# RWKV-7 attention with a hardswish feed-forward: third blocks of a group's inverses made in one unit instead of two

## Chip, cores and metric

The kernel runs on one core of one Trainium2 chip. The metric is the device time of one execution in microseconds (us). Each kernel is run several times; the median is given with the lowest and highest run. The profile comes from one further execution, whose own time is given beside its span. TensorE, VectorE, ScalarE, GpSimd and SyncE are called PE, DVE, ACT, POOL and SP, as in the profile; a line number such as L804 is one of the kernel before.

## The reference, cut to what matters

Attention with a state of 40 x 40 for each of 4 x 8 heads runs over 768 time steps; its output feeds a feed-forward layer from 320 to 2048 and back to 320 features. All data are float32.

```python
B, H, S, D = r.shape                     # 4, 8, 768, 40
for t in range(S):
    y[:, :, t] = einsum('bhd,bhde->bhe', rt, state)
    Sa = einsum('bhde,bhe->bhd', state, at)
    state = state * wt[:, :, None, :] - einsum('bhd,bhe->bhde', Sa, bt)
    state = state + einsum('bhd,bhe->bhde', vt, kt)
x = y.transpose(0, 2, 1, 3).reshape(B * S, H * D)     # 3072 x 320
h = x @ w_in                                          # 3072 x 2048
out = (h * clip(h + 3, 0, 6) / 6) @ w_out             # 3072 x 320
```

## The kernel before

**Units and groups.** The time axis is cut into blocks of 64 steps. A unit is one such block for two of the four batch entries, all 8 heads: it fills 128 partitions with two halves of 64 time steps. There are 24 units, in six groups of four (`NU = 4`). In each half of a unit, the 64 steps depend on each other through a triangular 64 x 64 matrix per head; its inverse `tinv` lets a unit be done with matmuls instead of step by step. The state is carried from unit to unit.

**The inverses.** They are made for a whole group at once, for 4 x 8 heads. `invert` (L744 on) takes the matrix `F` (written by ACT at L657 and L660), and inverts the two diagonal blocks of 32 x 32 on DVE, in some 60 small steps, dealt out one at a time by `aside` between other work. Its results are `tb` and, transposed, `tt`; the two diagonal blocks are copied into `tinv` at once (L790, L791). What is left is the third block, off the diagonal: a product of three 32 x 32 matrices, one after the other. That is `third_block` (L794 on). Each call serves two units of the group, 16 heads. Its first half is 32 small matmuls on PE, `F` times `tb` (L804), into a pair of PSUM banks, which ACT then copies to `zs` in four copies of 32 x 256 (L812). Its second half is 32 small matmuls of `tt` with `zs` (L827) into another pair of banks, copied by ACT into `tinv` in four copies (L837). In the trace each of these matmuls is two records, so that a set of 32 is a row of 64. Each half is a generator step: it yields once after its matmuls (`PE`), and once after its copies (`DONE`). `third_blocks` makes two of them, so that a group has four sets of matmuls and sixteen copies.

**The order of the work.** The instruction order of each engine is the order of the program text: the kernel schedules by hand. From the second group on, a unit is worked in four blocks (`BLOCKS = 4`, `j` from 0 to 3). `a_block` issues the attention stages of the current unit (`OWN_STAGES`) and those that prepare later units (`AHEAD_STAGES`), several stages together: first the matmuls of all, then the copies of all. `feed` puts pieces of the feed-forward of earlier units between them: `expand` (L1124, with `gt` made by ACT at L1139 and DVE at L1140) and `contract` (L1165). At the end of blocks 0 and 1 of the first two units of a group, `block` issues one half of a third block. `aside(3 * L)` before it runs what is left of `invert`. The stages that the prediction's steps touch, by block of a unit, are:

| block | stages and lines |
|---|---|
| 0 | RT and VT: R and V turned (L496, ACT L862, L895) |
| 1 | S (L906, ACT L911), R (PE L884, DVE L888), C (PE L524, DVE L546); with them A and B of a later unit (L496, DVE L615, L623) |
| 2 | U (L925, ACT L929) and UT (L964, ACT L970), which read `tinv`, and rS (L980, ACT L986); with them F, K of a later unit (L650, L486, L670, ACT L679) |
| 3 and 4 | H (L524), ysn (L1021, DVE L1028, L1032) |

The first unit needs the `tinv` of its own heads at block 2, thus one block after the second call of `block`.

**The banks.** PSUM has eight banks here: one called `one`, one `o`, two `h` for the feed-forward, and two pairs called `pair` (`ps_pair`, L141 on), which nearly all stages use in turn. A pair is taken again when its reader has emptied it, so a matmul into a pair waits for the copies of an earlier stage. `ps_pair` gives consecutive calls the same pair while both fit into its 512 columns and `shared[0]` has not been reset; a set of third-block matmuls takes 256 columns.

Of the kernel before, what the change touches and what calls it, by code (L numbers as in the profile page):

```python
# [20 lines left out]
L = 32  # L21
# [10 lines left out]
def kernel(  # L32
# [47 lines left out]
    NU = 2 * NP  # L80
# [762 lines left out]
    def third_blocks(first=False):  # L843

        zs = inv.tile([P, 2, 2, H, L], F32, name="zs", tag="x", bufs=1)
        return [third_block(*third[-1], 2 * n, zs[:, n], first) for n in range(2)]
# [360 lines left out]
    def aside(n, weight=0):  # L1207

        for _ in range(n):
            if side and next(side[0], side) is side:  # L1210
                side.popleft()
            due[0] += weight
            while due[0] >= 1:
                due[0] -= 1
                next(weights, None)

    def deal(n):

        for _ in range(n):
            next(weights, None)  # L1220

    def run(stage, steps=0, mixed=0, deals=0):

        for at in stage:
            if at == DONE:
                return
            aside(steps, mixed)
            deal(deals)
# [71 lines left out]
    blocks = {}  # L1300
# [28 lines left out]

    def block(i, j):  # L1330

        if i % NU < 2:
            if j == 0:
                if i % NU == 0:
                    blocks[i], blocks[i + 1] = third_blocks()
            run(blocks[i])

# [115 lines left out]
    def a_block(m):  # L1455

        if coming and begins[coming[0]] == m:
            u = coming.popleft()
            close = coming and begins[coming[0]] < m + BLOCKS
            ahead[u, m] = prepared(u), CLOSE_STAGES if close else AHEAD_STAGES  # L1460
        if m % BLOCKS == 0 and m // BLOCKS + NU < NK:
            i = m // BLOCKS + NU
            own[i, m] = step(i), OWN_STAGES
        parts = {}, {}
        for (u, begin), (fs, order) in sorted(own.items()) + sorted(ahead.items()):
            if m - begin < len(order):
                for name in order[m - begin]:
                    parts[begin % BLOCKS > 0].setdefault(name, []).append(fs[name])
        for k, part in enumerate(parts):
            together(part)  # L1470
            if any(u % NU == NU - 1 and m - begin == 2 and k == (begin % BLOCKS > 0)
                   for u, begin in ahead):
                third.clear()
                side.append(invert(group_F[-1], third))
            yield

    def feed(n, inversion):

        whole = int(n)
        for k in range(whole):  # L1480
            pieces(1)
            aside(inversion)
        pieces(n - whole)
# [3 lines left out]
    for i in range(NU, NK):  # L1487
        spread[0] = i >= 2 * NU - 1
        for j in range(BLOCKS):
            rate, inversion = 3.5, 0  # L1490
            if i + AHEAD >= NK + NU - 1:
                rate = 4.5
            if i < 2 * NU - 1:
                rate = 2.8
            parts = a_block(m)
            next(parts)
            if side or i % NU == NU - 1 and rate < 4:

                rate, inversion = 6.2, 2 + (i < 2 * NU)
            feed(rate / 2, inversion)  # L1500
            for _ in parts:
                pass
            if i % NU < 2 and j < 2:
                if i % NU == 0:
                    aside(3 * L)
                block(i, j)
            if side:
                rate, inversion = 6.2, 2 + (i < 2 * NU)
            feed(rate / 2, inversion)
            m += 1  # L1510
# [37 lines left out]
```

## Time and profile before

| | |
|---|---|
| median of 3 runs | 786.57 us (786.24 to 786.66) |
| profiled execution | 785.4 us |
| its span in the trace | 783.7 us |
| PE busy | 725.0 us, 93% of the span |
| DVE, ACT, POOL busy | 486.6, 320.2, 171.9 us |
| feed-forward matmuls L1124 and L1165 | 248.7 and 230.5 us busy, in 2304 and 768 records |
| third-block matmuls into `pair` (L804, L827) | 640 and 768 records of 0.19 us, overlapping |
| third-block copies (L812, L837) | 48 and 48 copies of 0.375 us |

A row of the timeline gives the start in us from the begin of the span, how long the row lasts from the start of its first to the end of its last instruction, the engine, the line, the operation, the tiles written and read, the shape, and the number of records that follow each other. A number in brackets is the time that the engine was idle ahead of the row, with the engine that ended it. Records of PE overlap, so the time that a row costs PE is from its start to the start of the next. The row of the stretches gives the length of the stretch, busy time of PE, of its weight load, and of DVE, ACT and POOL with their counts, then the granted clock, the DMA share and the bandwidth.

### The profile page before, as it was taken

The numbers are of one execution on the slowest core, as the hardware profiler recorded it, in microseconds if no ns is written. First come the engines' busy times: TensorE is split into PE (matmuls) and PEld (weight loads), VectorE is DVE, ScalarE is ACT, GpSimd is POOL, SyncE is SP. The second block draws the span as 40 slices with busy tenths as digits, with TensorE's granted clock in tenths as the row PEclk, the third lists the DMA queues.
The fourth block names the chain that finished last, engine by engine and source line by source line (L and its number), as shares of the span: only waits on it lengthen the run. The fifth ranks groups of instructions, "written<-read, shape, count | busy, mean of one in ns | idle before, by whom it ended". The sixth has DMA issues, their size and how long they took to land.

```text
span 783.7 us, 32780 instructions
## 1 busy us (share of the span) xinstructions
PE 725.0 (93%) x14552; PEld 613.3 (78%) x14552; DVE 486.6 (62%) x951; ACT 320.2 (41%) x664; POOL 171.9 (22%) x321
## 2 busy tenths in 40 slices
PE   5636788999999989999999999999999999999998
PEld 3625677878878778888788888888888888888886
DVE  7899967688546699345888336887436972223110
ACT  2386865324445334443334543334543234412211
POOL 6403111222232304121304212203212111110000
PEclk9855899999999999999999999999999999999999
DMA  9684554311333312223213223213221101110000
GB/s 123 116 202 123 113 168 69 68 27 35 58 59 63 67 33 48 50 49 66 41 38 58 46 51 64 44 30 60 49 55 39 26 5 30 30 29 10 12 20 18
DMA packets 174205, 44.87 MB, mean 57 GB/s; under 512 B 157424, under 2 KB 172784, under 8 KB 174064
## 3 DMA queue, kind: packets, MB, share of 16 engines
q1 hardware_dynamic: 169760, 42.03, 27.5%
q8 instruction: 115, 1.88, 1.0%
q10 hardware_dynamic: 4304, 0.74, 0.6%
q14 instruction: 26, 0.21, 0.1%
HBM read 34.08 MB, written 3.93 MB: 49 GB/s over the span
## 4 chain that ended last, share of the span: by engine, by line
PE 77%; DVE 10%; issue 6%; DMA 2%; ACT 2%; POOL 2%; SPq 1%; POOLq 0%; ACTq 0%; DVEq 0%
PE h L1124 27%; PE o L1165 25%; PE pair L1021 4%; PE pair L524 4%; PE pair L496 2%; PE one L486 2%; DVE prods L571 2%; PE pair L884 2%; PE pair L925 1%; PE pair L717 1%; DVE prod L769 1%; PE pair L964 1%; DVE x L775 1%; PE pair L980 1%; PE one L906 1%
## 5 line engine op out<-in xcount | busy, mean ns | idle before, releaser
L1124 PE MATMUL h<-xt,win 128*128 128x128 f32 (+1 forms) x2304 | 248.7, 281 | 4.5 <-DVE gt L1140 4.5
L1124 PEld LDWEIGHTS h<-xt,win 128*128 128x128 f32 (+1 forms) x2304 | 229.3, 191 | 22.6 <-issue 4.2
L1165 PE MATMUL o<-wout,gt 128*128 128x320 f32 x768 | 230.5, 443 | 0.0
L1165 PEld LDWEIGHTS o<-wout,gt 128*128 128x128 f32 x768 | 138.4, 190 | 50.9 <-issue 0.2
L1140 DVE SCALAR_TENSOR_TENSOR gt<-gt,h 128x512 f32<-128x512 f32 x96 | 62.0, 680 | 73.4 <-ACT gt L1139 73.4
L1139 ACT ACTIVATE gt<-h,three 128x512 f32<-128x512 f32 x96 | 62.9, 687 | 102.8 <-PE h L1124 102.3
L546 DVE COPY_PREDICATED area<-mask,pair 128x512 f32<-128x512 int32 x56 | 40.4, 724 | 62.2 <-PE pair L524 52.8
L769 DVE TENSOR_TENSOR prod<-x 128x30 f32<-128x30 f32 (+9 forms) x180 | 65.5, 364 | 8.9 <-POOL x L754 3.3
L775 DVE TENSOR_TENSOR x<-x,prod 128x30 f32<-128x30 f32 (+9 forms) x180 | 64.3, 357 | 5.5
L1029 POOL TENSOR_TENSOR yg<-ys,gam 128x512 f32<-128x512 f32 x20 | 25.4, 1272 | 126.1 <-DVE ys L1028 83.2
L690 POOL TENSOR_TENSOR KBt<-K,rgt 128x320 f32<-128x320 f32 x22 | 19.1, 870 | 151.4 <-ACT rgt L679 139.9
L571 DVE TENSOR_TENSOR_SCAN prods<-area,start 128x528 f32<-128x528 f32 x24 | 40.8, 1703 | 9.7 <-ACT area L567 9.6
L1028 DVE TENSOR_TENSOR ys<-pair,ys 128x512 f32<-128x512 f32 x20 | 13.8, 690 | 49.8 <-PE pair L1021 40.8
L862 ACT ACTIVATE RT<-pair 128x512 f32<-128x512 f32 x22 | 13.1, 597 | 54.5 <-PE pair L496 54.4
L722 ACT ACTIVATE EV<-pair 64x320 f32<-64x320 f32 x44 | 18.9, 430 | 36.9 <-PE pair L717 36.5
L1021 PE MATMUL pair<-area,KBt 64*64 64x104 f32 x1280 | 33.1, 252 | 0.0
L1183 ACT ACTIVATE ob<-o 128x320 f32<-128x320 f32 x22 | 9.6, 437 | 56.2 <-PE o L1165 37.8
L837 ACT ACTIVATE tinv<-pair 32x256 f32<-32x256 f32 x48 | 18.0, 375 | 34.7 <-PE pair L827 34.2
L582 DVE TENSOR_TENSOR_SCAN area<-area,start 128x528 f32<-128x528 f32 x24 | 31.1, 1297 | 0.8
L1021 PEld LDWEIGHTS pair<-area,KBt 64*64 64x64 f32 x1280 | 29.1, 133 | 1.4
L950 POOL COPY area<-V 128x320 f32<-128x320 f32 x20 | 9.1, 455 | 84.6 <-DVE area L612 52.9
L600 POOL COPY rgam<-prods 128x256 f32<-128x256 f32 x22 | 24.9, 1131 | 0.0
(286 smaller groups left out, 1049.9 us busy)
## 6 DMA issues: line engine op xcount, KB each, us to landing
V<-in_v_dram SPq DMA_DIRECT2D x96, 40.0 KB
out_dram<-ob SPq DMA_DIRECT2D x47, 80.0 KB
R<-in_r_dram SPq DMA_DIRECT2D x92, 40.0 KB
B<-in_b_dram SPq DMA_DIRECT2D x42, 80.0 KB
K<-in_k_dram SPq DMA_DIRECT2D x42, 80.0 KB
W<-in_w_dram SPq DMA_DIRECT2D x37, 80.0 KB
A<-in_a_dram SPq DMA_DIRECT2D x37, 80.0 KB
xt<-yg SPq DMA_DIRECT2D x72, 40.0 KB
```

Source lines behind the costliest of these rows:

```text
L524: nc.tensor.matmul(out=o[i][half(q), n ^ (2 * q * placed), :], lhsT=lhs[half(i, D), n ^ (2 * q * swap), half(q)], rhs=rhs[half(i, D), n, h ...
L546: nc.vector.copy_predicated(out=x[:].rearrange("p (i h) t -> p i h t", i=2), mask=mask8, data=o[2])
L571: nc.vector.tensor_tensor_scan(out=prods[:].rearrange("p r m i -> p (r m i)"), data0=wm[:, 0:SCAN], data1=start[:], initial=0.0, op0=ALU.m ...
L582: nc.vector.tensor_tensor_scan(out=back, data0=back, data1=start[:], initial=0.0, op0=ALU.mult, op1=ALU.add)
L769: nc.vector.tensor_tensor(out=pv, in0=_ap(x[:], (i + 1) * L + i, [[L, n], [0, i]]), in1=_ap(x[:], i * L, [[0, n], [1, i]]), op=ALU.mult,)
L775: nc.vector.tensor_tensor(out=rest, in0=rest, in1=pv, op=ALU.add)
L1021: nc.tensor.matmul(out=both[q][half(s), pr, :], lhsT=o[name][half(q), h * D:h * D + SLOT], rhs=beside[name][half(q), 4 * rs + 2 * (s ^ (q ...
L1029: nc.gpsimd.tensor_tensor(out=yg[:], in0=m["ys"][:].rearrange("p r q t -> p r (q t)"), in1=o["G"][:], op=ALU.mult)
L1124: nc.tensor.matmul(out=hp[c][:, i, :], lhsT=lhsT, rhs=rhs, start=(begun[c] == 0), stop=(begun[c] == 3 * NQ - 1))
L1139: nc.scalar.activation(out=gt[:], in_=hp[c][:], func=AF.Relu, bias=three[:], scale=1.0)
L1140: nc.vector.scalar_tensor_tensor(out=gt[:], in0=gt[:], scalar=6.0, in1=hp[c][:], op0=ALU.min, op1=ALU.mult)
L1165: nc.tensor.matmul(out=op[:], lhsT=gts[c][:, n, :], rhs=wout[:, c * HJ + r * NQ + n, :], start=((split or r == 0) and c == 0 and n == 0), ...
```

## The change

Both third blocks of a group are now made in the first unit: behind its block 0 the first halves of both, behind its block 1 the second halves. The matmuls of both come first, then the copies of both. The second unit has none. In the first unit PE thus issues 64 matmuls in a row at L804 and 64 at L827, and ACT eight copies in a row at L812 and eight at L837. Both sets fit into one pair of banks, so that each half takes one pair for four units where it took one for two. The first group, whose third blocks are made elsewhere, is not touched.

```diff
     def block(i, j):
 
-        if i % NU < 2:
-            if j == 0:
-                if i % NU == 0:
-                    blocks[i], blocks[i + 1] = third_blocks()
-            run(blocks[i])
+        if j == 0:
+            blocks[i] = third_blocks()
+        for x in blocks[i]:
+            next(x)
+        for x in blocks[i]:
+            run(x)
...
-            if i % NU < 2 and j < 2:
-                if i % NU == 0:
-                    aside(3 * L)
+            if i % NU == 0 and j < 2:
+                aside(3 * L)
                 block(i, j)
```

## Prediction

> **What bounds the kernel now.** I read the page first (busy shares, slices, chain of waits), then the busy time by stretches, then the timelines of TensorE (PE), ScalarE (ACT) and VectorE (DVE) around every third block (L804, L827), and last the order and the waits of the two programs as built, which hold no times.
>
> ```profile
> PE 725.0 (93%) x14552; PEld 613.3 (78%) x14552; DVE 486.6 (62%) x951; ACT 320.2 (41%) x664; POOL 171.9 (22%) x321
> PE 77%; DVE 10%; issue 6%; DMA 2%; ACT 2%; POOL 2%; SPq 1%; POOLq 0%; ACTq 0%; DVEq 0%
> ```
> ```profile
> 418.00:533.00 115.00, 113.97 (x2382) 97.46 (x2379) 75.50 (x148) 47.53 (x107) 27.26 (x48) 1.00 0.26 49
> ```
> PE carries the chain, and in the stretch of one group (418 to 533 us) it is busy 113.97 of 115.00 us at full granted clock. PE works in order, so what counts is how long its own list of matmuls is, plus each place where the next matmul waits. ACT is busy 41%: its share hides nothing here, since what matters is when its copies end.
>
> The third group shows what the change touches. First unit, PE and then ACT (start, us, what):
> ```profile
> 422.75 0.75 PE L804 MATMUL pair<-tb,F 32*32 32x32 f32 x64
> 423.43 1.16 PE L1124 MATMUL h<-xt,win 128*128 128x128 f32 x8
> ...
> 425.60 0.68 PE L884 MATMUL pair<-state,at 40*64 40x40 f32 x32
> ...
> 426.69 2.42 PE L1165 MATMUL o<-wout,gt 128*128 128x320 f32 x8
> 429.04 0.75 PE L827 MATMUL pair<-zs,tt 32*32 32x32 f32 x64
> ...
> 432.42 0.65 PE L980 MATMUL pair<-RT,S 40*64 40x64 f32 x32
> ```
> ```profile
> 423.66 1.54 ACT L812 ACTIVATE zs<-pair 32x256 f32<-32x256 f32 x4 [2.73 <-PE pair L804]
> 425.22 1.27 ACT L1139 ACTIVATE gt<-h,three 128x512 f32<-128x512 f32 x2
> ...
> 429.84 1.56 ACT L837 ACTIVATE tinv<-pair 32x256 f32<-32x256 f32 x4 [2.86 <-PE pair L827]
> ```
> Look at the margins. The zs copies end at 425.20, and L884, which is built to wait for them (it takes their two banks), starts at 425.60: 0.40 us to spare. The tinv copies end at 431.40, and L980, which takes the banks of L827, starts at 432.42: 1.02 us. Second unit, PE:
> ```profile
> 446.22 1.34 PE L1165 MATMUL o<-wout,gt 128*128 128x320 f32 x4
> 447.49 0.75 PE L804 MATMUL pair<-tb,F 32*32 32x32 f32 x64
> 448.18 1.34 PE L1165 MATMUL o<-wout,gt 128*128 128x320 f32 x4
> 449.36 1.05 PE L1124 MATMUL h<-xt,win 128*128 128x128 f32 x8
> ...
> 453.45 1.16 PE L1124 MATMUL h<-xt,win 128*128 128x128 f32 x8
> 454.87 0.74 PE L827 MATMUL pair<-zs,tt 32*32 32x32 f32 x64 [0.26 <-DVE area L612]
> 455.54 2.05 PE L1124 MATMUL h<-xt,win 128*128 128x128 f32 x16
> 457.43 0.60 PE L486 MATMUL one<-ident,K 128*128 128x128 f32 x4
> ```
> Here each block costs PE its 0.68 us and cuts a run of large matmuls in two.
>
> **The change, part by part.** Five groups (third blocks at about 192, 307, 423, 538 and 650 us). In the built order only PE and ACT differ; DVE, POOL and SP issue the same list, so no DMA moves in its queue.
>
> *Added in the first unit.* L804 and L827 are 128 records each instead of 64. Of the 0.75 us of a set, its last record is 0.19, so 63 steps take 0.56, 8.9 ns each: 64 more cost 0.57. Two per group: +1.14.
>
> *Taken out of the second unit.* Third group: 446.22 to 449.36 is 3.14 us; the same eight L1165 records without a break take 2.35 (426.69 to 429.04), so 0.79 goes. 453.45 to 457.43 is 3.98; 24 records of L1124 without a break take 2.88 (a piece of the chain of waits), so 1.10 goes, the 0.26 of waiting among it. The same way: second group 0.78 (329.59 to 333.80 against 3.43 for twelve) and 1.09; fourth 0.79 and 0.78; fifth 0.68 and 0.77; first 0.68 and 0.68, and 0.12 more where L980 at 228.28 waited for tinv copies that ended at 228.23.
>
> *The two waits, which grow.* All eight copies of a set stand in one ACT run, and the built program releases the first only after the last of both halves' matmuls. Four copies take 1.54 us, 0.388 from start to start, so four more cost 1.55. No row has eight in a run; I take the pitch of these same copies. The other row of 256 columns, L563 on 128 partitions, starts its successor after 0.27, so the four cost between 1.08 and 1.55, and I take 1.55, the row of the same shape; no row of 256 columns on ACT is slower. The zs end thus moves by 0.57 + 1.55 = 2.12, PE's own arrival by 0.57, and a release takes 0.05 or 0.06 (228.23 to 228.28). So the first wait is 1.61 less the margin, the second 1.55 + 0.06 less its margin:
>
> | group | zs end, waiting row, margin | first wait | tinv end, waiting row, margin | second wait |
> |---|---|---|---|---|
> | 1 | 195.00, L884 195.97, 0.97 | 0.07 | 200.97, L925 201.97, 1.00 | 0.60 |
> | 2 | 309.33, L884 309.85, 0.52 | 1.09 | 315.87, L980 316.74, 0.87 | 0.74 |
> | 3 | 425.20, L884 425.60, 0.40 | 1.21 | 431.40, L980 432.42, 1.02 | 0.59 |
> | 4 | 540.76, L884 542.23, 1.47 | 0.79 (below) | 547.26, L980 549.29, 2.03 | 0 |
> | 5 | 652.79, L827 656.11, 3.32 | 0 | 658.47, L980 660.12, 1.65 | 0 |
>
> In group 1 ACT is busy with earlier copies until 193.48, after the doubled L804 would end (193.2), so there the zs end moves by 1.55 alone. In group 1 all of U (L925) waits for all copies; elsewhere L925 waits for the first four and L980 for the last.
>
> Behind the zs copies on ACT stand two gt (L1139) and S (L911). DVE needs those gt for its own gt (L1140), and RR (L888) and the mask (L546), for which L827 waits, stand behind that. Group 4: the gt copies end at 542.05 + 2.12 = 544.17, DVE's second gt starts at 544.21, RR 0.60 later, L546 0.41 after that for 0.72, so it ends at 545.96 and L827 starts 0.14 later, 546.10 against 544.74: 1.36, of which 0.57 is work and 0.79 wait. In groups 2 and 3 the same walk ends at 314.5 and 430.4, before L827 would come (314.9 and 430.8). Behind L884 on PE stand L524 and the feed-forward matmuls; behind L980 the F products of the next group. All of it moves with PE, and I find no root that does not: the DVE stretch of the next inverses starts from F, which PE makes.
>
> *Sum.* Work 5 x 1.14 = 5.70, waits 3.16 + 1.93 = 5.09, taken out 1.48 + 1.87 + 1.89 + 1.57 + 1.45 = 8.26: +2.53 us. By group: +0.33, +1.10, +1.05, +0.36, -0.31. The profiled execution took 785.4 (span 783.7 and 1.7 around it): it becomes 787.9. The median of the runs, 786.57, lies 1.17 above: **789.1 us**.
>
> Two rules beside rows. A set of 64 records takes PE 0.68 us and its four copies take ACT 1.54. The Trainium skill, "TensorEngine Tiling (Array Packing)", section "PSUM Bottleneck", warns that tiles speed up the matmuls but not the emptying of PSUM, which may become the limit, and advises both ScalarE and VectorE for it: it speaks against bunching eight copies on ScalarE, and the two rows agree. The Trainium skill, "ScalarE: Activation LUTs", section "What ACT_TABLE_LOAD costs", gives 186 ns + 0.833 ns a column for such a copy and lets neighbours overlap by 93 ns, an estimate of 0.306 a copy of 256 columns. The rows say 0.388; by the page the waits would sum to some 3.0 and the change to about +0.5.
>
> **Rivals.**
> 1. *The copies are released early or the banks are not what L884 needs: no new wait.* Then 5.70 - 8.26 = -2.56 remains, **784.0**. The point that decides: zs must end within 0.4 us (group 3) to 0.5 (group 2) of where it does. For it: ACT idles 2.7 us ahead of the zs copies. Against it: both releases are in the built waits, and the margins are short. 10%.
> 2. *The added copies overlap as L563's do, 0.27 each.* Each wait is 0.47 shorter: 0.62, 0.74, 0.32 and 0.13, 0.27, 0.12, in all 2.20; sum -0.36, **786.2**. Against it: these copies have 0.388 in all rows; this is the direction of the page on ScalarE too, which those rows do not bear out. 5%.
> 3. *Later waits swallow part.* PE waits 0.77 at 391.29 and again at 506.84 for DVE's gt. If these do not move with PE, up to 0.77 is given back in groups 2 and 3: +1.0, **787.6**. Against it: that DVE run starts from what PE made. 15%.
> 4. *The delay spreads.* If in groups 2 and 3 L827 waits on DVE as in group 4, or UT (behind the longer tinv run on ACT) comes late, some 0.5 us more in four groups: +4.5, **791.1**. For it: the spare in that walk is only 0.3 to 0.4. 10%.
> That the change doesn't do what it says is ruled out by the built order.
>
> **How the numbers follow.** The forecast has 60%, with a range of its own of 788.1 to 790.2. The range over all reaches from rival 2 to rival 4, 786.2 to 791.1, and leaves out rival 1 and the far half of rival 4. A measurement of this kernel tells 0.2%, 1.6 us, from no change. Slower by more: forecast and rival 4, 0.70. Within: rivals 2 and 3, 0.20. Faster: rival 1, 0.10.
>
> **What would show it.** In the changed profile, in groups 2 and 3 of the blocks, an idle of about 1.1 to 1.2 us ahead of L884 put down to L812, and 0.6 to 0.7 ahead of L980 put down to L837; in group 1 0.6 ahead of L925; in group 4 one ahead of L827 put down to DVE. Each L812 and L837 row with x8 and 3.1 us. L804 and L827 rows of x128 taking 1.3 us, none in second units. In the fifth group no wait and a gain. If those idles are missing, the step on the waits is wrong; if they are there and the time stays, the step that all moves with PE is.

## The result and the profile after

The changed kernel takes 793.43 us (median of 4 runs, 792.8 to 794.07), the kernel before in the same comparison 786.4 us (median of 4, 783.97 to 786.66): a ratio of 1.0096, with a 95% interval of 1.0075 to 1.0118. It is slower, as forecast, but by 7.0 us where 2.5 were forecast, and it lies above the range. The profiled execution took 793.4 us with a span of 791.7; before it was 785.4 and 783.7. So the two traces that are compared here differ by 8.0 us.

The page of the kernel after, busy times and chain of waits:
```profile
PE 727.6 (92%) x14552; PEld 616.3 (78%) x14552; DVE 487.1 (62%) x951; ACT 321.0 (41%) x664; POOL 171.9 (22%) x321
PE 75%; DVE 6%; ACT 6%; issue 4%; SPq 4%; DMA 3%; POOL 1%; ACTq 0%; DVEq 0%; POOLq 0%
```
No engine has more instructions than before. PE is busy 2.6 us longer, so that some 5.4 of the 8.0 us are idle time. ACT's share of the chain rose from 2% to 6%, which is where the new waits would show. "Issue", time in which an engine waited for nothing that the profile shows, has 4% where it had 6%, and DVE 6% where it had 10%: the chain runs another way in part, so the page alone does not tell where the time went.

The first unit of the third group, PE and then ACT, as in the rows of before:
```profile
426.65 1.45 PE L804 MATMUL pair<-tb,F 32*32 32x32 f32 x128
...
431.28 0.68 PE L884 MATMUL pair<-state,at 40*64 40x40 f32 x32 [1.01 <-ACT zs L812]
...
434.72 1.50 PE L827 MATMUL pair<-zs,tt 32*32 32x32 f32 x128
...
439.66 0.69 PE L980 MATMUL pair<-RT,S 40*64 40x64 f32 x32 [0.52 <-ACT tinv L837]
```
```profile
428.14 3.08 ACT L812 ACTIVATE zs<-pair 32x256 f32<-32x256 f32 x8 [3.31 <-PE pair L804]
431.25 1.27 ACT L1139 ACTIVATE gt<-h,three 128x512 f32<-128x512 f32 x2
...
436.48 3.12 ACT L837 ACTIVATE tinv<-pair 32x256 f32<-32x256 f32 x8 [3.47 <-PE pair L827]
```
Both margins are gone. The zs copies end at 431.22 and L884 starts 0.06 later, after 1.01 us of idle. The tinv copies end at 439.60 and L980 starts 0.06 later, after 0.52. Eight copies take 3.08 and 3.12 us, twice what four took. The second unit, PE:
```profile
453.51 2.42 PE L1165 MATMUL o<-wout,gt 128*128 128x320 f32 x8
455.76 1.05 PE L1124 MATMUL h<-xt,win 128*128 128x128 f32 x8
...
459.86 2.94 PE L1124 MATMUL h<-xt,win 128*128 128x128 f32 x24
462.64 0.60 PE L486 MATMUL one<-ident,K 128*128 128x128 f32 x4
```
The runs of large matmuls are whole again: 2.25 us for the eight records where the cut run took 3.14, and 2.78 for the 24 where it took 3.98.

So far this is the forecast, and this group moves PE by 1.31 us against 1.05. The surprise stands in the first and the fourth group. The fourth, PE:
```profile
551.48 1.77 PE L827 MATMUL pair<-zs,tt 32*32 32x32 f32 x128 [0.72 <-DVE area L612]
553.18 0.54 PE L1165 MATMUL o<-wout,gt 128*128 128x320 f32 x1
554.80 3.77 PE L1165 MATMUL o<-wout,gt 128*128 128x320 f32 x7 [1.08 <-issue]
```
Right behind the long row PE issues one large record and then stands still for 1.08 us with nothing that holds it. And the seven records after that take 3.56 us to the next row, where seven of eight take some 2.0 elsewhere. The busy time by stretches says why (columns as in the section on the profile before; the granted clock is the third number from the end):
```profile
551.80:555.20 3.40, 2.32 (x116) 1.75 (x103) 0.72 (x2) 1.60 (x5) 0.18 (x2) 1.00 0.13 36
555.20:558.60 3.40, 3.40 (x9) 2.12 (x8) 0.00 (x0) 1.40 (x4) 0.00 (x0) 0.50 0.23 42
```
For 3.4 us PE is granted half its clock. The same happens in the first group, from 207.0 to 210.4. In the kernel before, no stretch from 167 us to the end of the span had less than the full clock.

Matching the PE rows of the two traces one by one gives the shift that each group adds:

| group | forecast | measured | of it not forecast |
|---|---|---|---|
| 1 | +0.33 | +2.49 | rows L804, L827 0.14 + 0.64 longer; half clock some 1.5 |
| 2 | +1.10 | +1.41 | rows 0.18 + 0.41 longer |
| 3 | +1.05 | +1.31 | rows 0.13 + 0.18 longer |
| 4 | +0.36 | +3.26 | rows 0.10 + 0.35 longer; idle behind L827 1.35; half clock 1.67 |
| 5 | -0.31 | -0.47 | L804 0.23 longer, L827 0.03 shorter |

"Longer" is from the start of a 128-record row to the start of the next, against the forecast of 1.25 us (0.68 + 0.57; where the row of before was longer, in one place each of groups 2 and 4, that plus 0.57). The ten rows add 2.33, the idle behind one of them 1.35, the half clock some 3.2.

### The profile page after: what moved, and what is told of

It is laid out like the page before. It is cut to its first block, busy times and chain, and to the rows that moved or that the text cites. A ratio compares the mean times of both kernels' runs of the same rounds, so it can differ in the third digit from the quotient of the medians.

```text
span 791.7 us, 32773 instructions
## 1 busy us (share of the span) xinstructions
PE 727.6 (92%) x14552; PEld 616.3 (78%) x14552; DVE 487.1 (62%) x951; ACT 321.0 (41%) x664; POOL 171.9 (22%) x321
## 3 DMA queue, kind: packets, MB, share of 16 engines
q8 instruction: 115, 1.88, 1.0%
## 4 chain that ended last, share of the span: by engine, by line
PE 75%; DVE 6%; ACT 6%; issue 4%; SPq 4%; DMA 3%; POOL 1%; ACTq 0%; DVEq 0%; POOLq 0%
PE h L1124 27%; PE o L1165 24%; PE pair L1021 4%; PE pair L524 4%; SPq L470 3%; PE one L486 2%; PE pair L496 2%; PE pair L884 2%; PE pair L717 1%; ACT tinv L837 1%; DVE prods L571 1%; PE pair L980 1%; PE pair L925 1%; PE pair L827 1%; ACT zs L812 1%
## 5 line engine op out<-in xcount | busy, mean ns | idle before, releaser
L1165 PE MATMUL o<-wout,gt 128*128 128x320 f32 x768 | 231.9, 446 | 1.1 <-issue 1.1
L1165 PEld LDWEIGHTS o<-wout,gt 128*128 128x128 f32 x768 | 139.6, 191 | 53.1 <-issue 2.6
L546 DVE COPY_PREDICATED area<-mask,pair 128x512 f32<-128x512 int32 x56 | 40.6, 725 | 67.8 <-PE pair L524 59.2
L1021 PE MATMUL pair<-area,KBt 64*64 64x104 f32 x1280 | 33.1, 252 | 0.0
L1021 PEld LDWEIGHTS pair<-area,KBt 64*64 64x64 f32 x1280 | 29.1, 133 | 1.4
L837 ACT ACTIVATE tinv<-pair 32x256 f32<-32x256 f32 x48 | 18.0, 375 | 18.0 <-PE pair L827 17.4
```

The lines of the kernel that those rows point to most:

```text
L546: nc.vector.copy_predicated(out=x[:].rearrange("p (i h) t -> p i h t", i=2), mask=mask8, data=o[2])
L837: nc.scalar.activation(out=tinv[z:z + L, heads, L:BL], in_=tp[x][z + y * L:z + y * L + L, part], func=AF.Copy)
L1021: nc.tensor.matmul(out=both[q][half(s), pr, :], lhsT=o[name][half(q), h * D:h * D + SLOT], rhs=beside[name][half(q), 4 * rs + 2 * (s ^ (q ...
L1165: nc.tensor.matmul(out=op[:], lhsT=gts[c][:, n, :], rhs=wout[:, c * HJ + r * NQ + n, :], start=((split or r == 0) and c == 0 and n == 0), ...
```

## A second theory for the rest

The theory on the waits (eight copies in a run hold the banks) covers the forecast part. For the other 6 to 7 us the trace of instruction transfers gives a theory. One DMA queue, marked "instruction", carries packets of 16,384 bytes (115 of them, 1.88 MB, in both kernels). PE's own instructions in the trace, matmuls, weight loads and semaphore operations, are 29,434: that is 256 a packet, 64 bytes each. A row of 128 records is 128 matmuls and 128 weight loads, thus one whole packet, and PE runs through it in 1.14 us at 8.9 ns a record. Behind 186 us a packet is on its way for 0.9 to 1.5 us in the kernel after (up to 1.6 before), so a new one is hardly brought faster than such a row uses it up. The **supply theory**: PE now runs out of instructions in or behind its 128-record rows; and where that leaves a stretch with little work on PE, the clock drops. What speaks for it is when the pauses end:

| kernel and pause | a packet landed | PE went on |
|---|---|---|
| after, in L827 of group 1 | 199.30 | 200.71, 1.41 later |
| after, behind L827 of group 4 | 553.41 | 554.80, 1.40 later |

The rivals to it are the forecast's own fourth case (waits on DVE that spread), the place (both blocks in the first unit), and the doubled sets costing PE more than 0.57 each without any pause.

## Experiments

All are compared with the kernel before, side by side on the same chip: 786.64 us (median of 19) for the first four, 787.15 (median of 8) for the last two.

**Copies alone.** Only the copies are doubled, in their old places, in both units; each stands once more with the same result.
```diff
-        for part in parts:
+        for part in parts * (1 if first else 2):
```
(in both halves)

> The kernel before, with each of the four copies of a third-block set (L812, L837) issued twice, outside the first group: bursts of eight copies on ACT, and rows of 64 matmul records on PE as before. My theory of the waits: four more copies take 1.55 us, so each wait is 1.61 less the margin in the trace of before. First units: 0.64, 1.09, 1.21, 0.77 (through DVE) ahead of L884 or L827 and 0.61, 0.74, 0.59 ahead of L925 or L980 in groups 1 to 4; second units 1.55 (group 1), 0.1, 0.1, 0.76, 1.34 ahead of L980 and 0.1 more. In all about +9.6 us, some 796 us, with no pause inside a row of L804 or L827; 1.5 us more for each stretch of half granted clock, if the waits alone can bring one on. Rival, that the copies cost little and the long rows on PE do all the harm: within 1 us of before.

Measured: 797.03 us (one run), 10.4 more. PE in the first unit of the third group:
```profile
431.17 0.68 PE L884 MATMUL pair<-state,at 40*64 40x40 f32 x32 [1.10 <-ACT zs L812]
...
437.58 0.30 PE L925 MATMUL pair<-RR,tinv 64*64 64x40 f32 x2 [0.51 <-ACT tinv L837]
438.47 0.80 PE L925 MATMUL pair<-RR,tinv 64*64 64x40 f32 x27 [0.59 <-ACT tinv L837]
```
Its list of waits from 186 to 783 us (us in total, times, longest):
```profile
PE pair L884 <- ACT zs L812: 3.6, 3, 1.2
PE pair L980 <- ACT tinv L837: 3.5, 3, 1.6
PE pair L925 <- ACT tinv L837: 3.2, 7, 0.6
```
These waits sum to 10.3 us, beside 10.4 more in all. No pause put down to "issue" stands in or behind the third-block rows and the clock stays full, though these waits are longer than those of the kernel after (2.0, 1.0 and 0.4 us in the same list). So waits of this kind alone do not bring the other losses. They cost more than expected, though: from 186 us to the end the PE rows shift by 13.6 us against the kernel before, not by 9.6. That the time is only 10.4 longer is luck: this one execution was 2.05 us ahead of the traced one of before at 186 us, and that one was 1.2 us faster than the median. Most of the excess stands ahead of L925 in the first units. The second copies write the same heads of `tinv` once more, so U probably has to wait for all eight, where in the change it needs only the first four; in this point the run is not the change.

**Sets alone.** Only the matmuls are doubled, in their old places; each set is issued twice with the same result.
```diff
-        for h in range(H):
+        for h in [*range(H)] * (1 if first else 2):
```
(for L804 and for L827)

> The kernel before, with each set of third-block matmuls (L804, L827) issued twice in a row, outside the first group: rows of 128 records on PE, twenty of them, and four copies a set on ACT as before. The second issue writes the same values. Theory that rows of 128 records run ahead of what feeds PE its instructions: pauses of 0.06 to 0.5 us inside the rows, as in the changed kernel, where ten rows cost 2.4 us over 0.57 each and one pause of 1.1 us came just behind a row. So 20 x 0.57 = 11.4 us of work and 4 to 8 us of pauses: 802 to 806 us. Rival, that the pauses come from the eight copies or from the shared banks: no pauses, 11.4 us, about 798 us.

Measured: 812.36 us (one run), 25.7 more: above both expectations. Twenty sets at 0.57 are 11.4. The list of waits names the rest:
```profile
PE pair L827 <- issue: 3.4, 4, 1.9
PE o L1165 <- issue: 2.4, 1, 2.4
PE pair L804 <- issue: 0.8, 2, 0.4
```
With two more of 0.5 and 0.4 these are 7.5 us of pauses, and three stretches of 3.41 us have half clock (from 440.0, 470.7 and 566.3). At some 1.6 for each of these, as in the kernel after, 23.7 of the 25.7 are named. No wait on zs or tinv has come. The largest pause inside a row, in the third group:
```profile
437.16 1.10 PE L827 MATMUL pair<-zs,tt 32*32 32x32 f32 x107
440.14 0.54 PE L827 MATMUL pair<-zs,tt 32*32 32x32 f32 x21 [1.89 <-issue]
```
The row stops after 107 of 128 records, in the middle of one set, where no semaphore is waited for; a packet landed at 438.85 and PE went on 1.29 later. The doubled sets alone bring pauses and half clock, without the place and without the longer copies. The sizes of the pauses were not forecast: what sets how long one lasts is how far the packets were behind, and I have no price for that.

**Place alone.** Both third blocks in the first unit, but one set of 64 records and four copies at a time: blocks 0 and 1 for the first pair of units, 2 and 3 for the second. Against the kernel before:
```diff
-        if i % NU < 2:
-            if j == 0:
-                if i % NU == 0:
-                    blocks[i], blocks[i + 1] = third_blocks()
-            run(blocks[i])
+        if j == 0:
+            blocks[i] = third_blocks()
+        run(blocks[i][j // 2])
...
-            if i % NU < 2 and j < 2:
-                if i % NU == 0:
+            if i % NU == 0:
+                if j < 2:
                     aside(3 * L)
-                block(i, j)
+                block(i, j)
```

> All third blocks of a group in its first unit as in the change, but one set at a time: the first pair of units' halves behind blocks 0 and 1, the second's behind blocks 2 and 3. No row over 64 records, no burst over four copies. Theory (bursts and long rows cost, not the place): within 1.5 us of before, 785 to 788 us, no pause in the rows and no new stretch of half clock. Rival, that work taken from the second unit to the first is what costs: 791 us or more.

Measured: 786.08 us (median of 10), ratio 0.999 [0.9974, 1.0007]: not to be told from the kernel before. The place costs nothing that these runs can tell. Two steps between records take 0.59 (in a row of L827) and 0.57 us (at L650) without a wait, which was not expected: rows of 64 can run short too when other short records stand close by. There is no half clock from 186 us to the last microsecond.

**Sets kept apart.** The four sets of the change, all in the first unit, with something between each two: the first half of pair 1 ahead of block 0's pieces of feed-forward, of pair 2 behind block 0, the second halves behind blocks 1 and 2. Against the kernel after:
```diff
-    def block(i, j):
+    def block(i, n):
...
-        if j == 0:
+        if i not in blocks:
             blocks[i] = third_blocks()
-        for x in blocks[i]:
-            next(x)
-        for x in blocks[i]:
-            run(x)
+        run(blocks[i][n])
...
+            if i % NU == 0 and j == 0:
+                aside(3 * L)
+                block(i, 0)
...
-            if i % NU == 0 and j < 2:
-                aside(3 * L)
-                block(i, j)
+            if i % NU == 0 and j < 3:
+                block(i, (1, 0, 1)[j])
```

> First unit again: the first half of the first pair of units ahead of the feed-forward pieces of block 0, that of the second pair behind block 0 as in the change, the second halves behind blocks 1 and 2. Rows of 64 records with large matmuls between, bursts of four copies. Theory: the early L804 waits for VT's copy to leave its banks, by the trace of before 0.95 us in group 2 and 0.2 in groups 3 and 4; else as before: 786.5 to 788.5 us, no pauses, no half clock past 200 us. Rival (place): 791 us or more.

Measured: 788.1 us (median of 10), ratio 1.0021 [1.0004, 1.0039], a time as expected. There are no waits on zs or tinv copies; L804, now earlier, waits 2.0 us in two groups for VT (L895), and two steps of 0.43 and 0.74 without a wait are left, where none was expected. The same sets and copies in the same unit cost some 5 us less than in the change (788.1 against 793.43) when no two sets and no eight copies stand together; this is waits, pauses and half clock in one, and doesn't divide them.

**First halves earlier.** The change, with the call behind block 0 moved ahead of its feed-forward pieces, so that these hide the zs copies. Against the kernel after:
```diff
+            if i % NU == 0 and j == 0:
+                aside(3 * L)
+                block(i, j)
...
-            if i % NU == 0 and j < 2:
-                aside(3 * L)
+            if i % NU == 0 and j == 1:
                 block(i, j)
```

> The change, with the first halves of both third blocks ahead of the feed-forward pieces of block 0 instead of behind them: the same rows of 128 and bursts of eight, but one to two pieces more of PE work between L804 and L884. Theory of three costs (waits for copies, pauses of PE's instruction supply, half clock): the first waits of the changed kernel go (0.2, 1.0, 1.0, 0.1 ahead of L884 and 0.7 ahead of L827); instead L804 waits for VT's copy, 1.0 in group 2, 0.2 in groups 3 and 4. Work -2.6, waits 1.4 + 1.5, so about +0.4 us against before without pauses; pauses of 2.5 to 3.7 us stay in the rows, at other records: 789 to 791 us, and 1.5 more for each stretch of half clock. Rival, that the waits for copies are no part of the loss: 793 us as in the change.

Measured: 795.33 us (median of 4), ratio 1.0091 [1.0062, 1.012]: a miss, it is no faster than the change. The idle ahead of L884 did go in groups 2 to 4 (0.68 is left in group 1), but L804 came to stand behind 64 records of L1021 and 16 of L496, all short, and ran dry sooner. The fourth group, PE:
```profile
544.81 1.35 PE L804 MATMUL pair<-tb,F 32*32 32x32 f32 x118
547.73 0.28 PE L804 MATMUL pair<-tb,F 32*32 32x32 f32 x10 [1.57 <-issue]
```
The pauses put down to "issue" at L804 sum to 3.4 us and one at L1165 is 1.8, and the clock is half from 208.9 for two stretches. I had meant to take the first wait away and nothing else; the edit changed the supply as well, so it says nothing on the price of the waits. It does fit the supply theory, which I had not applied to what stands ahead of the row.

**Packets shifted.** The change, with one set of the first group (at some 63 us, far ahead of the rows in question) issued twice. These 128 PE instructions are half a packet: behind them each row meets the packets at another point, and nothing else is edited.
```diff
-        for h in range(H):
+        for h in [*range(H)] * (2 if first and n == 0 else 1):
```
(for L804 alone)

> The change, with one set of third-block matmuls of the first group (into the borrowed banks, at about 63 us) issued twice: 128 more PE instructions early on, half of what one 16 KB packet of the instruction queue holds, and 0.6 us of work. Theory that the pauses come from the supply of instructions: the places where the supply runs out move, so the pauses of 0.53 us in the second row of group 1 and of 0.35 and 1.1 us at that of group 4 go or move to other rows; each pause over 0.4 us that no wait explains ends 1.2 to 1.6 us after a packet of that queue landed; time between 789 and 796 us. Clock: a stretch of 3.41 us whose matmuls stream fewer than some 1230 full-array columns (columns x rows x columns of the tile / 128 squared) is followed by half clock, none over 1340 is. Rival, that the pauses belong to the place (banks, transfers of data): the same rows pause for the same time, +0.6 us.

Measured: 792.26 us (median of 5, 789.4 to 793.41), ratio 1.0054 [1.0033, 1.0076]. The profiled execution is the fastest of them, 789.4. Its fourth group, PE:
```profile
550.69 1.51 PE L827 MATMUL pair<-zs,tt 32*32 32x32 f32 x128 [0.72 <-DVE area L612]
552.12 2.42 PE L1165 MATMUL o<-wout,gt 128*128 128x320 f32 x8
```
Same rows, same wait for DVE, but the 1.08 us of idle behind L827 and the half clock are gone; the pause in L827 of the first group is gone as well (1.31 instead of 1.89), and no pause in any of the ten rows is over 0.16 us. The waits stayed:
```profile
PE pair L884 <- ACT zs L812: 2.3, 2, 1.2
...
PE pair L980 <- ACT tinv L837: 0.6, 2, 0.4
```
From 192 us to the end, PE's rows shift by 2.8 us against the kernel before: the +2.53 of the forecast. This is strong evidence for the supply theory, since work and waits are nearly those of the change (0.6 us of work more, far ahead) and the place of the packets' borders differs. It holds for the profiled execution. In the medians little is gained (792.26 against 793.43 for the change, measured at another time); the other runs of this kernel, up to 793.41, have no trace, and the likely reason of their spread, that packets land at other times in each run, is an inference.

Over all kernels, each such step of over 0.4 us from one PE record to the next that no wait explains ended 1.2 to 1.6 us after an instruction packet had landed: 19 pauses in five kernels, the two of the table above among them.

The traces show more than this nearness in time. Number PE's matmuls, weight loads and semaphore operations from 0 in the order of their start. Then all 19 pauses end at a matmul with the number 256 N + 193 or 256 N + 194, where N is the number of instruction packets that had landed by then. The two of the table are 26 x 256 + 194, 1.41 us behind packet 26, and 83 x 256 + 194, 1.40 behind packet 83. Nor does the record with the number 256 N + 193 start less than 1.2 us behind the landing of packet N anywhere in the eight traces from 186 us on. So PE stands each time at the border between two packets, whatever the line, and goes on when the next one is there.

One idle time of 1.5 us at L717 is also put down to "issue". It stands in every kernel, the one before too, with a number close to such a border, but there packet N had landed some 10 us before. With the numbers shifted by 128 it stands at 256 N + 63 and lasts as long. In the kernel before it ends 0.1 us behind a DVE copy at L546, so I take it for a wait on DVE.

The border does not explain everything, however. Of the 2.33 us by which the ten rows of the kernel after are longer, some 0.7 stand at a border (0.5 in group 1, 0.15 in group 5); the rest is steps of 0.06 to 0.17 us at other numbers. Most of what is left in the packets-shifted kernel is of this kind too. What makes these short steps stays open.

No faster version came out: the best, sets one at a time in the first unit, has an interval that holds 1.

## Why the prediction was right in direction and wrong in size

**Added in the first unit: the step that failed.** The forecast stretched a 64-record row at 8.9 ns a record to 128 and took 0.57 for each doubling, 5.70 in all. Where nothing runs short that is what a doubling costs: 0.54 in the fifth group (1.22 against 0.68). But the step took for granted that PE's instructions are there. Nine of the ten rows took longer, and one was followed by 1.35 us of idle: 3.7 us more. Some 2.0 of it stand at borders between packets, and missing instructions are shown as their cause; the other 1.7 are the short steps whose cause is open. In the packets-shifted kernel some 1.1 of the 3.7 stays and 2.6 goes. The trace of before could have warned: a row of 64 is half a packet, and the row of instruction packets stood on the page with its bytes and count.

**The path is PE's list at full clock: failed in two places.** The forecast read the granted clock of 1.00 in one stretch before and kept it. Two stretches of half clock cost some 3.2 us. They followed on stretches with little work in the array, as the last section shows. Only the one in group 4 follows on a pause at a packet border. In the stretch ahead of the other, PE idles 1.10 us for UT (L970), as in the kernel before, and 0.37 for tinv.

**The two waits: right.** The forecast had 5.09 us, the shifts of the rows sum to some 5.0: first waits 0.10, 1.08, 1.08, 0.86 (0.21 at L884 and 0.65 at L827), 0 against 0.07, 1.09, 1.21, 0.79, 0; second waits 0.44, 0.72, 0.71, 0, 0 against 0.60, 0.74, 0.59, 0, 0. The doubled copies alone show waits of this kind without the rest, but at another price. The estimate from the Trainium skill, "ScalarE: Activation LUTs", section "What ACT_TABLE_LOAD costs", 0.306 a copy, is not borne out: eight copies in a run take 3.08 and 3.12 us, 0.385 to 0.39 each.

**Taken out of the second unit: a little too small.** 9.07 against 8.26: the last large record ahead of a cut is longer by some 0.1 as well, which the comparison with a whole run missed. It offsets a part of the longer rows.

**The rivals.** Released early (784.0) and overlapping copies (786.2) fall with the idles ahead of L884 and L980 and with the 3.1 us rows. Swallowed later (787.6) falls too: the waits for DVE's gt still take 0.77 and have moved with PE. "The delay spreads" (791.1) was nearest in time, by another mechanism: beyond the one forecast at L827 of group 4, no new wait on DVE or UT came.

**The sum.** Work 5.7 + waits 5.0 - taken out 9.1 + longer rows and the idle behind one 3.7 + half clock 3.2 = 8.5, against 8.0 between the two profiled executions. Of the rest, -0.5, some 0.4 stands in group 4: two rows of L650 that took 0.98 and 0.81 us before take 0.65. Each held a short pause at a packet border (steps of 0.24 and 0.16 us), which is gone. So the kernel before ran short as well, only less. The forecast added 1.17 from the profiled execution to the median; here the profiled 793.4 is the median, which is why the medians miss by 4.3 and the traces by 5.5.

## What to carry to other kernels

Count the instructions of a run of small matmuls and not its microseconds alone: where 256 of them go by in little over a microsecond, bunching two runs costs more than twice one, and the same run with large matmuls between its halves costs less. When moving work on PE, look at what short records stand next to its new place. And where a profile shows idle time put down to "issue", set the landing times of the instruction packets beside it before looking for a wait.

## What the runs showed of the hardware

**Instructions come in packets, and PE can outrun them.** 16,384 bytes for 256 PE instructions, 0.9 to 1.6 us on the way, and 1.2 to 1.6 us from landing to the next matmul where PE had run dry. Rows of 128 records (256 instructions in 1.14 us) paused for up to 1.9 us (sets alone), each pause over 0.4 us at the border of a packet.

**The clock was halved behind stretches with little work in the array; their idle time does not tell them apart.** This stretch of the kernel before is followed by full clock, though PE is idle in 44% of it:
```profile
279.10:282.50 3.40, 1.91 (x44) 1.70 (x43) 3.33 (x9) 0.47 (x2) 0.51 (x2) 1.00 0.14 41
```
The stretch 551.80 to 555.20 of the kernel after, shown above, is idle in 32% and followed by half. So is the one in its first group, idle in 43%:
```profile
203.60:207.00 3.40, 1.93 (x92) 1.65 (x95) 0.69 (x1) 2.01 (x6) 0.00 (x0) 1.00 0.03 7
207.00:210.40 3.40, 3.40 (x69) 3.28 (x62) 0.00 (x0) 1.85 (x5) 1.68 (x2) 0.50 0.03 4
```
In the kernel with first halves earlier, the stretch from 557.1 to 560.5 is even idle in 52% and full clock follows. The difference is in the tiles. For each stretch of 3.41 us I summed, over the records of PE that start in it, the columns streamed times the share of the 128 x 128 array that the tile covers. The stretch before has 1472 (large tiles), the one after 1146 (mostly 32 x 32). Over eight kernels, from 186 us on and among stretches at full clock, all six with at most 1256 are followed by half clock, and none with 1312 or more is (the table gives those six and some of the next). A large record at the edge of a stretch moves its sum by up to 320, so the border is not as sharp as these numbers look:

| sum in the stretch | kernel, start | next stretch |
|---|---|---|
| 534, 896, 1020 | sets alone, 436.6, 467.3, 562.9 | half |
| 1146, 1256 | after, 551.8, 203.6 | half |
| 1158 | first halves earlier, 205.5 | half |
| 1312 | first halves earlier, 427.4 | full |
| 1336 | sets alone, 224.9 | full |
| 1412 | packets shifted, 205.2 | full |
| 1472 | before, 279.1 | full |

A stretch full of 128-column records on the whole array, at 0.116 us each (24 in 2.78), would have some 3,770, so the border lies near a third of it. I made the rule on the first six traces and the last two (first halves earlier, packets shifted) agree with it; no experiment moved the sum alone. How a clock that is already half comes back stays open: a half-clock stretch with 1592 was followed by full, one with 1594 by half.

The Trainium skill, "TensorE: Matmul & The Clock Gate", section "HAM oscillation — how this bites in real kernels", puts the rule as no idle gaps of PE of over some 3.4 us. These traces agree with the length of the stretch, 3.41 us, but not with that bound: the longest idle times in the stretches ahead of the two half-clock ones of the kernel after were 1.1 us each.
